# Storing a batch's ninth tokens by one transfer of 128 partitions, its DRAM side ordered half of the columns, token, column

## The chip, the cores and the metric

The kernel runs on one core of a Trainium2 chip. The metric is the device time of one execution in microseconds; lower is better. A core has a matrix engine (TensorE, PE in the profile, with its weight loads as PEld), three engines for elementwise work (VectorE or DVE, ScalarE or ACT, GpSimd or POOL), a SyncE (SP) that here issues nearly all transfers, and 16 DMA engines that move the data.

## The reference: thresholded attention, then a maxout feed-forward layer

```python
scores = scale * q @ k.T                       # 8 batches, 8 heads, 576 tokens, 64 columns
thresh = max(scores) - tau                     # by row
attn = softmax(where(scores >= thresh, scores, -1e9))
x = (attn @ v) with the heads side by side     # 4608 x 512
h = maximum(x @ w1, x @ w2, x @ w3)            # 4608 x 768
out = h @ w_out                                # 4608 x 512, float32
```

## The kernel before

A batch's 576 tokens are taken as 64 groups of 9: token 9p + c is number p of chunk c. Two chunks (c = 0 to 7) fill 128 rows, so a batch has four chunk pairs of 128 tokens and a ninth chunk (c = 8) of 64 tokens. Four heads are a "quad"; 8 batches of two quads give 16 quads.

For each quad q, k and v are loaded (`load`, lines 185-237) and q and k turned on TensorE (tiles tp, qt, kt). For each of nine steps the scores of 128 rows go to PSUM (`scores`, tile sc). VectorE takes the maximum, ScalarE and VectorE make the exponents and sums (tile z), GpSimd divides by the sums into a bf16 tile P (`normalized`, six buffers). A DMA transpose on SyncE's queue brings P's two heads into ptq (`turned`, lines 400-404), nine of them for a quad. When all nine have landed, TensorE multiplies ptq with v (`product`, lines 406-441, PSUM tile o, then xt). The last batch is taken in two parts, the first with only some of the steps.

The feed-forward layer of a batch (`ffn`, from line 466) has three steps. `hid` multiplies xt with the three weights (tiles ph, hm, hT). `outp` (lines 511-542) multiplies hT with w_out for two chunk pairs at a time (tile po), ScalarE copies 128 x 512 values to a buffer ob (four buffers) and SyncE stores 256 KB; the very last of these goes out on ScalarE's queue (q10 in the profile; SyncE's is q1). `ninth` (lines 544-565) does the same for the 64 ninth tokens: columns 0 to 255 of the output are made in PSUM rows 0 to 63 and columns 256 to 511 in rows 64 to 127, so ScalarE copies 128 x 256 values, to a buffer obr (two buffers). Row 64x + p of obr is thus half x of token p's row.

The order of all work is written out by hand in the string ORDER (lines 40-74), a letter for each piece, and `_Ordered` (lines 84-101) keeps each engine to it; that is why nearly every instruction of the profile carries line 93. N issues a ninth chunk's matmuls, j its copy, i its stores, and o a 256 KB store. Each of N, j and i occurs eight times, and the string ends with stores, i the last. The `store` of `ninth` is put off by way of the list stores9 until its i. A transfer waits, ahead of its issue on SyncE, for its data, and everything behind it in SyncE's order waits along.

Of the kernel before, what the change touches and what calls it, by code (L numbers as in the profile page):

```python
# [104 lines left out]
def kernel(  # L105
# [23 lines left out]
    tensor, scalar, vector, pool, sync = (  # L129
        _Ordered(tc, e) for e in (nc.tensor, nc.scalar, nc.vector, nc.gpsimd, nc.sync))  # L130
# [50 lines left out]
    def bank(name, where):  # L181
        return ps_s.tile([128, 1024], F32, name=name, tag=f"s{where}")
# [261 lines left out]
    def halves(banks):  # L444


        mine = []

        def issue(swap):
            if swap:  # L450

                gate = tensor.nop()
                tc.add_manual_dep(gate.ins, mine[0], mybir.DependencyInfo(mybir.DependencyClass.Sync, mybir.DependencyReason.DATA), reason="swap")
            for ms in zip(*banks):
                for h in (1, 0):
                    x = (1 - h) ^ swap
                    o, w, m = ms[x]
                    rows = slice(64 * h, 64 * h + 64)
                    last = tensor.matmul(o, w(rows), m(rows), start=(not swap and ms[x] is banks[x][0]),
                                         stop=(swap == 1 and ms[x] is banks[x][-1]))  # L460
            if not swap:
                mine.append(last.ins.name)

        return (lambda: issue(0)), (lambda: issue(1))

    def ffn(b, part):


        runs = ((0, S // 2), (S // 2, S)) if part is None else (span(part),)
        mine = [c for c in (part or range(5)) if c < 4]  # L470
        chunks = [tuple(mine[c:c + 2]) for c in range(0, len(mine), 2)] + ([4] if part is None or 4 in part else [])
        st = {}
        nr, n = len(runs), runs[0][1] - runs[0][0]

        def hid(f, wi):
            my = {}

            def operands(kc, a):
                c0, c1 = runs[a]
                return (my["ps"][:, a * 512:a * 512 + n],  # L480
                        lambda rows: wts[wi][rows, kc, f * 128:(f + 1) * 128],
                        lambda rows: x_of(b)[rows, kc, c0:c1])

            def first(where):
                my["ps"] = bank("ph", where)
                if nr == 1:
                    for kc in range(4):
                        o, w, m = operands(kc, 0)
                        tensor.matmul(o, w(slice(0, 128)), m(slice(0, 128)), start=(kc == 0), stop=(kc == 3))
                else:  # L490
                    my["h"] = halves([[operands(kc, a) for kc in range(4)] for a in range(2)])
                    my["h"][0]()

            def done():
                if wi == 0:
                    st["hm", f] = hp_.tile([128, nr, n], BF16, name="hm", bufs=3)
                hm = st["hm", f]
                pv = my["ps"].rearrange("p (a u) -> p a u", a=2)[:, :nr, :n]
                if wi == 0:
                    scalar.activation(out=hm, in_=pv, func=AF.Copy)  # L500
                else:
                    dst = hm if wi == 1 else \
                        h_of(b)[:, f, runs[0][0]:runs[-1][1]].rearrange("p (a u) -> p a u", a=nr)
                    vector.tensor_tensor(out=dst, in0=pv, in1=hm, op=OP.max)
            p = _Piece((b, part, f, wi), first, (lambda: my["h"][1]()) if nr == 2 else None, [done])
            p.kind = "v" if wi else "h"
            return p

        rows_out = out[b * S:(b + 1) * S, :].rearrange("(p c) m -> p c m", c=9)

        def outp(cs):

            my = {}
            c = cs[0]
            last = b == B - 1 and cs[-1] == 3

            def first(where):
                ps = bank("po", where)
                my["ps"] = two = [ps[:, 0:512], bank("po", (where + 2) % 4)[:, 512:1024] if last else ps[:, 512:1024]]
                if len(cs) == 1:  # L520
                    for f in range(NF):
                        tensor.matmul(ps[:, 0:512], h_of(b)[:, f, c * 128:c * 128 + 128], wo[:, f, :],
                                      start=(f == 0), stop=(f == NF - 1))
                    return
                my["h"] = halves([[(two[a],
                                    lambda rows, a=a, f=f: h_of(b)[rows, f, (c + a) * 128:(c + a) * 128 + 128],
                                    lambda rows, f=f: wo[rows, f, :]) for f in range(NF)] for a in range(2)])
                my["h"][0]()

            def done(a):  # L530
                ob = hp_.tile([128, DM], F32, name="ob", bufs=4)
                src = my["ps"][a]
                if last and a == 1:
                    vector.tensor_copy(out=ob, in_=src)
                    ends.append(lambda: scalar.dma_start(out=rows_out[:, (0, 2, 1, 3)[c + a]:8:4], in_=ob))
                    return
                scalar.activation(out=ob, in_=src, func=AF.Copy)
                stores.append(lambda: sync.dma_start(out=rows_out[:, (0, 2, 1, 3)[c + a]:8:4], in_=ob))
            p = _Piece((b, "out", c), first, (lambda: my["h"][1]()) if len(cs) == 2 else None,
                       [lambda a=a: done(a) for a in range(len(cs))])  # L540
            p.kind = "uf" if last else "u"
            return p

        def ninth():

            my = {}

            def first(where):
                my["ps"] = ps = bank("po", where)
                for f in range(NF):  # L550
                    for x in range(2):
                        tensor.matmul(ps[64 * x:64 * x + 64, :256], h_of(b)[:, f, 512:S], wo[:, f, 256 * x:256 * x + 256],
                                      start=(f == 0), stop=(f == NF - 1))

            def done():
                ob = hp_.tile([128, DM // 2], F32, name="obr", bufs=2)
                scalar.activation(out=ob, in_=my["ps"][:, :256], func=AF.Copy)

                def store():
                    for x in range(2):  # L560
                        sync.dma_start(out=rows_out[:, 8, 256 * x:256 * x + 256], in_=ob[64 * x:64 * x + 64])
                stores9.append(store)
            p = _Piece((b, "ninth"), first, None, [done])
            p.kind = "j"
            return p

        return ([hid(f, wi) for f in range(NF) for wi in range(3)],
                [outp(c) for c in chunks if c != 4], [ninth() for c in chunks if c == 4])
# [9 lines left out]
    def span(part):  # L578
        if part is None:
            return 0, S  # L580
        return 128 * part[0], S if part[-1] == 4 else 128 * part[-1] + 128
# [11 lines left out]
    def x_of(b):  # L593
        if b not in xts:
            xts[b] = xp.tile([128, 4, S], BF16, name="xt")
        return xts[b]

    def h_of(b):
        if b not in hTs:
            hTs[b] = hp_.tile([128, NF, S], BF16, name="hT")  # L600
        return hTs[b]
# [120 lines left out]
    x = 0  # L722
# [39 lines left out]
```

## Time and profile before

| | us |
|---|---|
| median of 3 runs | 449.69 (449.37 to 450.16) |
| the profiled execution | 448.81 |
| its span, first instruction to last | 447.0 |
| TensorE busy | 427.8 |
| ScalarE busy | 404.5 |
| VectorE busy | 391.4 |
| GpSimd busy | 310.7 |
| stores of obr | 16 of 64 KB, median 2.2 from issue to landing |
| DMA transposes | 144, median 4.6 from issue to landing |

All rows but the first are of one profiled execution. A row of the profile names the engine, the operation, and out<-in by the program's tiles; "SPq" is SyncE's sequencer, which issues transfers and waits. "Landing" is when a transfer's last completion is counted. The DMA view of a stretch of time counts the packets of all 16 DMA engines by size, and gives for each queue the time that its packets took as a share of 16 engines over the stretch; its row of digits is the busy share in tenths in 40 equal slices. The windows view gives the busy time of each engine in a stretch, then the granted clock of TensorE, the DMA share and GB/s.

### The profile page before, as it was taken

The page shows a single profiled execution, that of the slowest core. Times are in us where ns is not written, and L with a number is a line of the kernel's source. Part 1 is how long each engine was busy: PE and PEld are TensorE (multiplying, and loading weights), DVE is VectorE, ACT ScalarE, POOL GpSimd, SP SyncE. Part 2 cuts the span into 40 slices and gives each one's busy share as a digit, 9 for nine tenths or more (in the row PEclk, how much of TensorE's full clock was granted, in tenths as well). Part 3 has the DMA queues.
Part 4 walks back from the last instruction along what each step waited for, and adds up shares of the span by engine and source line. Part 5 has one row for each costly group of instructions (what it writes and reads, how often), then busy time and mean ns, then how long its engine had stood idle before and what let it go on. Part 6 is the DMA issues. An engine that isn't in the chain of part 4 may idle for free.

```text
span 447.0 us, 14312 instructions
## 1 busy us (share of the span) xinstructions
PE 427.8 (96%) x5188; PEld 320.1 (72%) x5188; DVE 391.4 (88%) x1225; ACT 404.5 (90%) x841; POOL 310.7 (70%) x420
## 2 busy tenths in 40 slices
PE   8777799999999999999999999999999999999995
PEld 6443545887787777788687776787688876786862
DVE  4988899989899999999899899999999998998542
ACT  3999999998999999999999999999999999898422
POOL 2799789998667875876767776687748784657200
PEclk9987789999999999999999999999999999999999
DMA  7999999999999999999989989989999996995812
GB/s 177 317 228 203 258 207 230 213 194 279 198 218 170 233 202 207 217 261 166 164 232 180 270 133 231 171 167 219 177 263 158 236 179 93 169 166 112 149 73 107
DMA packets 212840, 87.46 MB, mean 196 GB/s; under 512 B 185889, under 2 KB 199713, under 8 KB 212769
## 3 DMA queue, kind: packets, MB, share of 16 engines
q1 hardware_dynamic: 212320, 85.98, 96.2%
q8 instruction: 41, 0.67, 0.6%
q10 hardware_dynamic: 448, 0.56, 0.4%
q14 instruction: 31, 0.25, 0.2%
HBM read 34.60 MB, written 9.44 MB: 99 GB/s over the span
## 4 chain that ended last, share of the span: by engine, by line
PE 84%; ACT 5%; DVE 3%; POOL 3%; DMA 1%; issue 1%; SPq 1%; DVEq 0%; POOLq 0%
PE ph L93 32%; PE sc L93 30%; PE po L93 10%; PE o L93 9%; ACT z L93 4%; PE tp L93 3%; DVE z L93 2%; POOL P L93 2%; DMA qm<-in_q_dram 1%; SPq L93 1%; POOL qs L93 1%; DVE kt L93 0%; ACT qt L93 0%; POOL vb L93 0%; DVE stage L93 0%
## 5 line engine op out<-in xcount | busy, mean ns | idle before, releaser
L93 POOL TENSOR_SCALAR P<-z,rs 128x576 bf16<-128x576 f32 x250 | 197.8, 803 | 71.6 <-DVE rs L93 37.0
L93 DVE TENSOR_SCALAR_CACHE_REDUCE z<-sc 128x576 f32<-128x576 f32 x250 | 182.0, 752 | 19.8 <-PE sc L93 11.1
L93 PE MATMUL sc<-kt,qt 64*128 64x320 f32 (+2 forms) x640 | 184.0, 442 | 5.6 <-DVE z L93 3.2
L93 PE MATMUL sc<-kt,qs 64*128 64x256 f32 (+2 forms) x640 | 183.1, 430 | 6.2 <-ACT z L93 2.8
L93 PE MATMUL ph<-xt,w 64*128 64x288 bf16 (+2 forms) x2160 | 164.4, 283 | 0.0
L93 PEld LDWEIGHTS <-w 64*128 64x128 bf16 (+1 forms) x2160 | 127.0, 94 | 27.0 <-issue 4.2
L93 PEld LDWEIGHTS sc<-kt,qs 64*128 64x128 f32 (+1 forms) x640 | 95.7, 183 | 30.5 <-ACT z L93 7.5
L93 ACT ACTIVATE z<-z 128x576 f32<-128x576 f32 x170 | 114.6, 678 | 0.1
L93 PEld LDWEIGHTS sc<-kt,qt 64*128 64x128 f32 (+1 forms) x640 | 95.5, 183 | 20.9 <-DVE z L93 6.7
L93 ACT ACTIVATE z<-z,th 128x576 f32<-128x576 f32 x134 | 99.8, 769 | 2.3 <-DVE rs L93 1.5
L93 DVE SCALAR_TENSOR_TENSOR z<-z 128x576 f32<-128x576 f32 x80 | 62.9, 801 | 0.3 <-ACT z L93 0.3
L93 POOL COPY qs<-qt 64x640 f32<-64x640 f32 (+3 forms) x66 | 45.6, 691 | 14.5 <-ACT qt L93 11.1
L93 ACT ACTIVATE z<-z,nm 128x576 f32<-128x576 f32 x71 | 53.5, 767 | 0.0
L93 PE MATMUL po<-wo,hT 64*128 64x512 bf16 (+1 forms) x480 | 53.2, 356 | 0.1
L93 ACT ACTIVATE hm<-ph 128x576 bf16<-128x576 f32 (+2 forms) x54 | 31.8, 590 | 14.9 <-PE ph L93 14.6
L93 DVE TENSOR_TENSOR hm<-ph,hm 128x576 bf16<-128x576 f32 (+2 forms) x54 | 37.0, 686 | 9.4 <-PE ph L93 8.7
L93 POOL TENSOR_SCALAR P<-stage,rs 128x576 bf16<-128x576 f32 x38 | 29.9, 793 | 18.2 <-DVE rs L93 7.5
L93 PEld LDWEIGHTS <-hT 64*128 64x128 bf16 (+1 forms) x480 | 28.8, 97 | 17.0 <-issue 2.1
L93 DVE TENSOR_TENSOR hT<-ph,hm 128x576 bf16<-128x576 f32 (+2 forms) x54 | 37.1, 687 | 3.8 <-PE ph L93 1.3
L93 PE MATMUL o<-ptq,vb 128*64 128x64 bf16 (+2 forms) x544 | 38.6, 282 | 0.0
L93 ACT ACTIVATE z<-sc,nm 128x576 f32<-128x576 f32 x45 | 32.1, 746 | 4.3 <-DVE z L93 4.2
L93 ACT ACTIVATION_READ_ACCUMULATOR z<-z 128x1 f32 x170 | 33.4, 197 | 0.0
(42 smaller groups left out, 410.7 us busy)
## 6 DMA issues: line engine op xcount, KB each, us to landing
vm<-in_v_dram SPq DMA_DIRECT2D x32, 256.0 KB, 5.3
out_dram<-ob SPq DMA_DIRECT2D x31, 256.0 KB, 4.3
qm<-in_q_dram SPq DMA_DIRECT2D x15, 512.0 KB, 4.5
km<-in_k_dram SPq DMA_DIRECT2D x15, 512.0 KB, 5.3
stage<-in_moe_w_dram SPq DMA_DIRECT2D x9, 512.0 KB, 4.8
ptq<-P SPq DMA_TRANSPOSE x144, 4.6
stage<-in_moe_w_out_dram SPq DMA_DIRECT2D x3, 512.0 KB, 5.3
vr<-in_v_dram SPq DMA_DIRECT2D x32, 32.0 KB, 2.9
```

The source lines that it names most:

```text
L93: ins = fn(*a, **kw)
```

## The change

In `ninth`, the two stores of 64 partitions each (half x of the columns from rows 64x to 64x + 63 of obr) become one of all 128 partitions. Its source is the whole of obr; its destination is the same piece of the output, read in the order half of the columns (2), token (64), column (256). The bytes and where they go are the same, and so is everything else in the program: on every engine but SyncE the instructions stand in the same order as before, and on SyncE each pair of obr stores is one.

```diff
                 def store():
-                    for x in range(2):
-                        sync.dma_start(out=rows_out[:, 8, 256 * x:256 * x + 256], in_=ob[64 * x:64 * x + 64])
+                    sync.dma_start(out=rows_out[:, 8].rearrange("p (x m) -> x p m", x=2), in_=ob)
                 stores9.append(store)
```

Here `rows_out` is a batch's 576 output rows as [64 groups, 9, 512 columns]. A row of a half is 256 float32 values, 1 KB in one piece; neighbouring tokens of the chunk lie 18 KB apart in DRAM, and the two halves of a token 1 KB.

## The prediction

> **What bounds the kernel now.** I read the page first: the span, the busy shares and the chain that ended last.
>
> ```profile
> span 447.0 us, 14312 instructions
> PE 427.8 (96%) x5188; PEld 320.1 (72%) x5188; DVE 391.4 (88%) x1225; ACT 404.5 (90%) x841; POOL 310.7 (70%) x420
> ...
> PE 84%; ACT 5%; DVE 3%; POOL 3%; DMA 1%; issue 1%; SPq 1%; DVEq 0%; POOLq 0%
> ```
>
> TensorE is busy for 96% of the span and makes 84% of the chain; a transfer can matter in two ways only, by making TensorE wait or by standing behind its last work. The changed store stands there, so I read the chain near its end, then the timeline and the tile obr for the same stretch, and SyncE's waits.
>
> ```profile
> 442.62 0.38 ACT obr L93
> ```
>
> ```profile
> 442.54 0.54 SPq L93 DMA_DIRECT2D out_dram<-ob  x1
> 442.62 0.38 ACT L93 ACTIVATE obr<-po 128x256 f32<-128x256 f32 x1
> 442.68 0.64 ACTq L93 DMA_DIRECT2D out_dram<-ob  x1
> 443.17 1.28 SPq L93 DMA_DIRECT2D out_dram<-obr  x2
> ```
>
> ```profile
> L93 SPq DMA_DIRECT2D out_dram<-obr x2: 552/614/675, 443.2 to 443.8; - x2
> ...
> DMA to landing us min/median/max: 2.2/2.4/2.7
> ```
>
> ```profile
> SPq L757 <- DMA out_dram<-obr: 1.5, 1, 1.5
> ```
>
> The last arithmetic is the copy of the last batch's ninth tokens out of PSUM. It ends at 443.00, SyncE issues the two stores at 443.17 and 443.78, and they land 2.7 and 2.2 us later, at 445.9 and 446.0. SyncE waits 1.5 us for them, and the span ends 1.0 us after the landing. So **the last pair of stores is on the path that sets the end**, microsecond for microsecond. The other seven pairs are issued while TensorE works.
>
> **The change part by part.** It removes eight of SyncE's issues and leaves the bytes, the packets and the arithmetic as they are: still 64 + 64 rows of 1 KB. What it alters is the shape of the output side, which now begins with a dimension of 2 in place of one of 64. How a transfer is dealt out to the 16 DMA engines can be counted where nothing else runs, in the DMA view of 438 to 447 us, with six stores (four of 256 KB, two of 64 KB).
>
> ```profile
> DMA packets 737, 1.20 MB, mean 133 GB/s; under 512 B 96, under 2 KB 224, under 8 KB 736
> ```
>
> The 224 - 96 = 128 packets of 1 KB are the two small stores' rows, 736 - 224 = 512 of 2 KB the other four's. The 96 tiny ones are 16 for each of the six transfers, one for each engine: a store of 64 rows is dealt 4 rows to an engine, one of 128 rows 8. Each of them leads with 64 or 128 on both sides, which 16 divides; so does every other transfer of the kernel. The new store leads with 128 in SBUF and with 2 in DRAM, and no row shows such a one. The ends are 16 engines, as in these rows, and 2, one for each leading piece. The rows are nearer to 16, but they share just the property that the change takes away: with 16 engines, one side's leading dimension would have to be cut in mid-dimension to keep both sides in step. I take **2 engines**, and keep 16 as a rival.
>
> The Trainium skill, "DMA: Bandwidth & Descriptors", section "Why a DMA increments its semaphore by 16 and not by 1", says that a transfer issued by SyncE uses the largest number of engines up to 16 that divides the slowest dimension (other than 1) of both sides. The 16 small packets for each transfer agree with it; for 128 and 2 it gives 2. No run here shows that case yet.
>
> **At the end.** What do 64 rows on one engine cost? Two stretches hold such packets nearly alone: 445.15 to 446 us, behind the last stores, and 383.7 to 385 us, with a pair in mid-run.
>
> ```profile
> DMA packets 143, 0.11 MB, mean 129 GB/s; under 512 B 36, under 2 KB 143, under 8 KB 143
> ...
> q1 hardware_dynamic: 139, 0.11, 40.4%
> ```
>
> ```profile
> DMA packets 167, 0.13 MB, mean 102 GB/s; under 512 B 39, under 2 KB 167, under 8 KB 167
> ...
> q1 hardware_dynamic: 167, 0.13, 39.3%
> ```
>
> In the first, 107 rows took at most 0.404 x 16 x 0.85 = 5.5 us, 51 ns each, the tiny packets counted in; I take 48 for a row alone. In the second, 128 rows took 0.393 x 16 x 1.3 = 8.2 us, 64 ns each. So 64 rows on one engine take 3.1 us (64 x 48 ns) to 4.1 us (64 x 64), where the 8 of now take 0.4. They queue behind the two 256 KB stores of the timeline, as the DMA view of 443.6 to 447 shows:
>
> ```profile
> DMA  0489999999999999998999300000000000000000
> ...
> q1 hardware_dynamic: 304, 0.39, 32.3%
> q10 hardware_dynamic: 144, 0.26, 20.8%
> ```
>
> A slice is 0.085 us. The engines are busy from 443.69 to 445.6 without a gap; each has 0.323 x 3.4 = 1.10 us of q1 and 0.208 x 3.4 = 0.71 us of q10. With 0.4 of it gone and 3.1 put in, the two engines are done at 443.69 + 1.81 - 0.4 + 3.1 = 448.2, where the last is done at 445.6 now: 2.6 us later, and 3.6 by 64 ns. The two needn't be the ones that are last now, so I take **2.5 us**. The issue that goes (0.61 us, the median above) brings nothing there: the first of the pair is issued at the same 443.17, and its rows wait for the engines. If nothing stood ahead of them, rows could start at most 445.1 - 444.4 = 0.7 us earlier (1.2 us behind the issue, as the 442.54 store's behind its own), so the smallest gain in time, with all rows at 48 ns, would be a loss of still 1.9 us.
>
> **In mid-run.** Each of the seven other stores puts 56 rows more, 2.7 us (56 x 48 ns), on two engines, and what is issued next lands later by up to that, less 0.6 us of issue saved. What follows are DMA transposes, for which TensorE's products wait. The tightest place is the second pair:
>
> ```profile
> 307.39 1.99 SPq L93 DMA_DIRECT2D out_dram<-obr  x2
> 309.49 7.09 SPq L93 DMA_TRANSPOSE ptq<-P  x5
> ```
>
> ```profile
> DMA to landing us min/median/max: 3.3/3.6/5.3
> ```
>
> ```profile
> 321.24 1.15 PE L93 MATMUL o<-ptq,vb 128*64 128x512 bf16 x16
> ```
>
> ```profile
> 309.00:317.00 8.00, 8.00 (x95) 5.24 (x93) 7.67 (x25) 8.00 (x18) 4.44 (x7) 1.00 1.06 199
> ```
>
> The middle row is that of the transposes issued from 309 to 320 us. The five take 1.42 us each (7.09 / 5), so the fifth is issued at about 315.2 (309.49 + 4 x 1.42) and landed by 320.5 at the latest (5.3 us); its product starts at 321.24, so 0.7 us of cover. The DMA share of 1.06 says that the engines have no slack there to work off a backlog. At the worst 2.7 - 0.6 (issue) - 0.7 (cover) = 1.4 us reach TensorE; at the best nothing, as the two engines catch up whenever they finish a transpose in less than SyncE's 1.42 us. I take 0. Elsewhere the cover is larger:
>
> ```profile
> 237.86 1.24 SPq L93 DMA_DIRECT2D out_dram<-obr  x2
> 239.20 3.32 SPq L93 DMA_TRANSPOSE ptq<-P  x2
> ```
>
> ```profile
> 251.09 0.65 PE L93 MATMUL o<-ptq,vb 128*64 128x512 bf16 x6
> ```
>
> ```profile
> 389.43 1.24 SPq L93 DMA_DIRECT2D out_dram<-obr  x2
> 390.77 1.27 SPq L93 DMA_TRANSPOSE ptq<-P  x1
> 392.14 0.59 SPq L93 DMA_DIRECT2D out_dram<-ob  x1
> 392.82 3.17 SPq L93 DMA_TRANSPOSE ptq<-P  x2
> ```
>
> ```profile
> 401.49 0.63 PE L93 MATMUL o<-ptq,vb 128*64 128x256 bf16 x8
> ```
>
> ```profile
> 420.97 2.53 SPq L93 DMA_DIRECT2D out_dram<-obr  x4
> 423.54 1.89 SPq L93 DMA_DIRECT2D out_dram<-ob  x3
> ```
>
> Behind the first pair the transposes are issued by 242.5, and with the 5.3 us from above they land by 247.8, 3 us ahead of their product; behind the pair at 389.43 the first two, which the product at 401.49 reads, are issued by 394.4 and land by 399.7, 1.8 us ahead by the worst landing. The two pairs from 420.97 have only stores behind them, which no arithmetic reads; the two obr buffers are written again only by the second ninth chunk after.
>
> **Sum.** 2.5 us at the end, 0 in mid-run: a span of 449.5 in place of 447.0, and 451.3 in place of the profiled execution's 448.81 (1.8 us lie around its span). That execution was 0.9 us below the median of the runs, 449.69; I put the same step on the median: **452.2**.
>
> **Rivals.** *All 16 engines, not slower.* If the transfer is dealt out by its 128 rows, each engine gets the same 8 rows as now, one issue of 0.61 us goes, and the end stays with engines that are busy to 445.6 anyway: 0 to 0.6 us gained, 449.1 to 449.7, likeliest 449.5. It decides at one point: whether the last landing stays at 446.0 or earlier. For it speak the 16 packets of each transfer in the row above, against it that none leads with fewer than 16. A sentence of the Trainium skill speaks for such a gain: "DMA: Bandwidth & Descriptors", section "Rules for kernel authors", advises one 128-partition transfer in place of two on disjoint halves of the partitions, as both halves use the same engines. The rows agree in that both stores of a pair use all 16, but the rule takes for granted that the merged one does too.
>
> *The backlog reaches TensorE.* As the forecast, and at 321.24 up to 1.4 us more, with as much again where several delays meet (389 us): 453.5 to 455. For it speaks the DMA share of 1.06, against it the covers above.
>
> *The rows are slower on two engines.* 64 ns a row instead of 48: 453.2. It is the upper end of the forecast.
>
> *It is cut into the two old transfers again*, with both issues: 449.7.
>
> **How the numbers follow.** Forecast with its own range 451.2 to 453.4: 0.72. Backlog on TensorE: 0.13. Sixteen engines: 0.12, two thirds of it within 0.2%. Cut in two: 0.03. The range, 451.2 to 454.8, takes in the first and the second and leaves out 0.15 for the cases near 449.5. A measurement of this kernel tells about 0.2% (0.9 us) from no change. Faster by more: 0.03; within: 0.12; slower by more: 0.85.
>
> **What would show it.** In the window of the last five stores the tiny packets fall from 96 to 4 x 16 + 2 = 66 with two engines, to 80 with sixteen. The last obr store takes about 5.2 us to land instead of 2.2 to 2.7, and SyncE's last wait for it grows from 1.5 to about 4.6 us. The product at 321.24 starts with no wait for ptq. I am wrong if the last landing stays near 446.0, or if the last copy of obr, at 442.62, comes later by over 0.5 us.

## The result, and the profile after

The changed kernel takes **453.23 us** (median of 10 runs, 451.17 to 456.36) against 449.75 (10 runs, 448.47 to 450.22): ratio **1.0082**, 95% interval 1.0057 to 1.0108. It is slower by 2.6 to 4.9 us. The profiled execution took 453.22 us, with a span of 451.4.

The page after, its span and busy shares, and the chain's shares:

```profile
span 451.4 us, 14301 instructions
PE 427.2 (95%) x5188; PEld 320.3 (71%) x5188; DVE 390.6 (87%) x1225; ACT 404.3 (90%) x841; POOL 309.6 (69%) x420
...
PE 84%; ACT 6%; POOL 3%; DVE 2%; DMA 2%; issue 1%; SPq 0%; POOLq 0%; DVEq 0%
```

No engine has more work: TensorE's busy time is 427.2 us where it was 427.8, yet the span is 4.4 us longer. So look at the end. The timeline behind the last matmuls:

```profile
443.65 0.38 ACT L93 ACTIVATE obr<-po 128x256 f32<-128x256 f32 x1
443.65 0.64 ACTq L93 DMA_DIRECT2D out_dram<-ob  x1
444.20 0.54 SPq L93 DMA_DIRECT2D out_dram<-obr  x1
```

and what SyncE waited for in the same stretch:

```profile
SPq L756 <- DMA out_dram<-obr: 5.6, 1, 5.6
```

The copy ends at 444.03 and the span at 451.4: 7.4 us, where it was 443.00 to 447.0, 4.0 us. SyncE's wait for the last store grew from 1.5 to 5.6 us. The DMA view of 440 to 452 us, with its busy digits and GB/s in slices of 0.3 us, says why:

```profile
DMA  0200006979910001999990111011111000000000
GB/s 0 55 0 0 0 0 239 396 273 362 416 62 0 0 0 48 362 416 403 403 120 17 27 21 24 34 48 48 48 48 48 34 24 14 0 0 0 0 0 0
DMA packets 707, 1.20 MB, mean 100 GB/s; under 512 B 66, under 2 KB 194, under 8 KB 706
```

Five stores left 66 tiny packets: 16 for each of the four stores of 256 KB and **2 for the merged store**. Its 194 - 66 = 128 rows are the plateau at the right: digit 1 (two engines of sixteen) and 48 GB/s falling to 24, where one engine is done, after 400 GB/s for the stores ahead of it.

The other 1.0 us of the longer span is there before the change can act. The first matmuls of three products, at 122, 200 and 424 us, after:

```profile
122.52 1.22 PE L93 MATMUL o<-ptq,vb 128*64 128x512 bf16 x15
...
200.99 1.18 PE L93 MATMUL o<-ptq,vb 128*64 128x512 bf16 x16
...
425.57 0.63 PE L93 MATMUL o<-ptq,vb 128*64 128x256 bf16 x8
```

and before:

```profile
122.34 1.22 PE L93 MATMUL o<-ptq,vb 128*64 128x512 bf16 x15
...
199.95 1.18 PE L93 MATMUL o<-ptq,vb 128*64 128x512 bf16 x16
...
424.54 0.63 PE L93 MATMUL o<-ptq,vb 128*64 128x256 bf16 x8
```

After is 0.18 us late at 122, 1.04 at 200 and 1.03 at 424. The first changed store is issued at 238.6 us, behind all of that delay; from there on, through seven merged stores, TensorE loses nothing. The product that the prediction called the tightest, at 321.24 before, is 1.03 us late too and waits for nothing:

```profile
322.27 1.16 PE L93 MATMUL o<-ptq,vb 128*64 128x512 bf16 x16
```

### The profile page after: what moved, and what is told of

It reads as the page before. It is cut to its first block, busy times and chain, and to the rows that moved or that the text cites. A ratio compares the mean times of both kernels' runs of the same rounds, so it can differ in the third digit from the quotient of the medians.

```text
span 451.4 us, 14301 instructions
## 1 busy us (share of the span) xinstructions
PE 427.2 (95%) x5188; PEld 320.3 (71%) x5188; DVE 390.6 (87%) x1225; ACT 404.3 (90%) x841; POOL 309.6 (69%) x420
## 4 chain that ended last, share of the span: by engine, by line
PE 84%; ACT 6%; POOL 3%; DVE 2%; DMA 2%; issue 1%; SPq 0%; POOLq 0%; DVEq 0%
PE ph L93 31%; PE sc L93 31%; PE po L93 10%; PE o L93 9%; ACT z L93 5%; PE tp L93 3%; DMA qm<-in_q_dram 2%; POOL P L93 2%; DVE z L93 1%; POOL qs L93 1%; DVE kt L93 0%; ACT qt L93 0%; SPq L93 0%; POOL vb L93 0%; DVE stage L93 0%
```

## The experiments

Theory A: the whole loss is the last store, dealt to two engines, on the path to the end; the seven in mid-run are covered. The main rival, B: the seven hold up DMA transposes and TensorE waits for them. "The end" below is the time from the end of the last copy of obr to the end of the span, 4.0 us before and 7.4 after. It is the sharpest measure: within one kernel's runs the whole times differ by 1.8 us and more.

**Only the last store merged** (e1_last_only) and **only the first seven** (e2_first_seven), each against before:

```diff
-                    for x in range(2):
-                        sync.dma_start(out=rows_out[:, 8, 256 * x:256 * x + 256], in_=ob[64 * x:64 * x + 64])
+                    if b == B - 1:      # e2: if b < B - 1
+                        sync.dma_start(out=rows_out[:, 8].rearrange("p (x m) -> x p m", x=2), in_=ob)
+                    else:
+                        for x in range(2):
+                            sync.dma_start(out=rows_out[:, 8, 256 * x:256 * x + 256], in_=ob[64 * x:64 * x + 64])
```

> Only the last of the eight ninth stores is one transfer; the first seven stay pairs. Theory A (the whole loss is the last store, dealt to two engines, on the path to the end; the seven in mid-run are covered): as the changed kernel, 3.0 to 3.8 us over before, about 453.1. Rival B (the seven delay transposes and TensorE waits, the last store is only a part of the loss): 1 to 2.5 us over before. In the DMA view of the last 11 us the tiny packets are 66 by both.

> The first seven ninth stores are one transfer each, the last stays a pair. Theory A: as before, within 0.5 us of 449.75. Rival B: 1 to 2.5 us over before, with TensorE's waits for ptq, or the distance between the two kernels' matmuls, growing behind one of the stores.

The last alone: 453.97 us against 449.53, ratio 1.0102 (1.0079 to 1.0126); the end 7.3 us, with 66 tiny packets. The first seven alone: 449.72, ratio 1.0007 (0.9985 to 1.0029); the end 4.1 us. The spans and the last copies of the two, the last alone first:

```profile
span 451.7 us, 14311 instructions
...
443.96 0.38 ACT L93 ACTIVATE obr<-po 128x256 f32<-128x256 f32 x1
```

```profile
span 447.0 us, 14302 instructions
...
442.50 0.38 ACT L93 ACTIVATE obr<-po 128x256 f32<-128x256 f32 x1
```

In the profile of the first seven alone, the first products behind the first and the second merged store (before, at 251.09 and 321.24):

```profile
250.97 1.18 PE L93 MATMUL o<-ptq,vb 128*64 128x512 bf16 x16
...
321.12 1.16 PE L93 MATMUL o<-ptq,vb 128*64 128x512 bf16 x16
```

Both are 0.12 us early, as this execution was already at 200 us (199.83): between and behind two merged stores nothing was lost.

Theory A holds for the place of the loss, and B falls: the last store alone costs 3.6 to 5.7 us by the interval, the seven nothing that can be told from zero. In size A gave 3.0 to 3.8 us; the end is 3.3 us longer (7.3 - 4.0), but the medians differ by 4.4. That profile was 1.4 us late before 200 us, with no changed instruction until 444. Whether such a delay makes the rest of the medians' difference too isn't shown.

**How many engines: 61, 62 and 60 tokens in the last pair** (e3_last_61, e3_last_62, e3_last_60), to see what decides it without any leading 2:

```diff
+                    n = 61 if b == B - 1 else 64      # 62, 60
                     for x in range(2):
-                        sync.dma_start(out=rows_out[:, 8, 256 * x:256 * x + 256], in_=ob[64 * x:64 * x + 64])
+                        sync.dma_start(out=rows_out[0:n, 8, 256 * x:256 * x + 256], in_=ob[64 * x:64 * x + n])
```

> The last pair stores 61 of its 64 tokens, in two transfers of 61 partitions (three tokens of the last batch are left out of the output). Theory A in its narrow form (a transfer uses the largest number of engines up to 16 that divides its leading dimension): 61 has no divisor but 1, so both transfers, 122 rows, run on one engine: 122 x 48 ns = 5.9 us, to 122 x 56 = 6.8, where 8 rows take 0.4: 5.2 to 6.4 us over before, and 4 x 16 + 2 x 1 = 66 tiny packets in the last 11 us. Rival C (it was the 2 pieces of the output side; rows are shared out over 16 engines as evenly as they go): as before, 96 tiny packets.

> The last pair stores 62 of its 64 tokens, two transfers of 62 partitions (two tokens of the last batch are left out of the output). Theory A: 62 gives 2 engines, 31 rows each, 62 on each engine for the pair: the end like the merged store's, 6.5 to 7.5 us from the last copy's end to the end of the span (7.4 with one transfer), 3 to 4 us over before, 68 tiny packets in the last 11 us. Rival C (the cost comes of the output side's leading 2, not of the number of engines): as before, 4.0 us behind the last copy.

> The last pair stores 60 of its 64 tokens, two transfers of 60 partitions (four tokens of the last batch are left out of the output). Theory A (the largest divisor up to 16 of the leading dimension): 60 gives 15 engines, 4 rows each: the end as before, 4.0 us from the last copy's end to the end of the span, and 4 x 16 + 2 x 15 = 94 tiny packets in the last 11 us. Rival C (any leading dimension that 16 doesn't divide drops to one or two engines): 6 to 10 us behind the last copy.

The packet counts of the last stretch, with 61, 62 and 60 tokens (the DMA views of 440 to 457, 438 to 452 and 438 to 449 us):

```profile
DMA packets 701, 1.19 MB, mean 70 GB/s; under 512 B 66, under 2 KB 188, under 8 KB 700
```

```profile
DMA packets 705, 1.19 MB, mean 85 GB/s; under 512 B 68, under 2 KB 192, under 8 KB 704
```

```profile
DMA packets 727, 1.19 MB, mean 108 GB/s; under 512 B 94, under 2 KB 214, under 8 KB 726
```

With 64 of them for the four larger stores, 2, 4 and 30 are left for the two small ones: 1, 2 and 15 engines each, the largest divisors up to 16 of 61, 62 and 60.

| last store | engines | the end, us | median, us | ratio to before beside it (interval) |
|---|---|---|---|---|
| pair of 64 (before) | 16 | 4.0 | | |
| pair of 60 | 15 | 3.9 | 449.82 | 0.9991 (0.9974 to 1.0008) |
| pair of 62 | 2 | 7.8 | 453.44 | 1.0079 (1.0056 to 1.0103) |
| merged (after) | 2 | 7.4 | 453.23 | 1.0082 (1.0057 to 1.0108) |
| pair of 61 | 1 | 10.3 | 457.03 | 1.0166 (1.0134 to 1.0198) |

So it is the number of engines and not the merging or the leading 2 as such: one token fewer than 62 costs 2.5 us more at the end, two fewer cost nothing against before. All three expectations of C fall. Theory A held for the engines in each; in size, the pair of 62 was 0.3 us over the end forecast for it, and the pair of 61 has an end 6.3 us longer than before's, within the 5.2 to 6.4 forecast, but a median 7.5 us over its before of 449.53 (its profile was 3.4 us late at 200 us).

The Trainium skill's rule that the prediction named ("DMA: Bandwidth & Descriptors", "Why a DMA increments its semaphore by 16 and not by 1") agrees with all five counts.

**Twice the dose in mid-run** (e5_seven_61): the same edit with `if b < B - 1` and 61, so that each of the first seven pairs puts 122 rows on one engine.

> The first seven pairs store 61 of 64 tokens each (three tokens of seven batches are left out of the output); the last pair is whole. A test of the cover in mid-run with twice the dose: if 61 rows go to one engine, each pair puts 122 x 48 = 5.9 us on one engine where the merged store put 3.1 on each of two. Theory A with the covers of the prediction: the product behind the second pair has 0.7 us of cover, so up to 5 us of wait there, with catching up 1 to 5 us over before in all. Rival D (a backlog on one engine in mid-run is hidden whatever its size): within 0.5 us of before.

457.91 us, ratio 1.0182 (1.0151 to 1.0213): 6.8 to 9.6 us, more than either expectation. The end is 4.0 us, and the profile, 0.96 us behind before's at 200 us, is 9.12 behind it at 424: 8.2 us arise in mid-run. TensorE's waits for transfers from 237 us on and the product behind the second pair, whose first matmul before is at 321.24:

```profile
PE o L93 <- DMA ptq<-P: 4.0, 3, 2.2
PE tp L93 <- DMA qm<-in_q_dram: 1.5, 1, 1.5
```

```profile
323.91 0.38 PE L93 MATMUL o<-ptq,vb 128*64 128x512 bf16 x1
325.88 0.44 PE L93 MATMUL o<-ptq,vb 128*64 128x512 bf16 x3 [1.58 <-DMA ptq<-P]
```

The product starts, waits 1.58 us for a transpose and goes on. After and the first seven alone have no such wait from 237 us to the end. So the cover is real and finite: 64 rows on each of two engines fit under it, 122 on one don't. Rival D falls. The place called the tightest makes only 1.8 us of the loss; 1.7 are lost behind the first pair, where TensorE waits for a load of q (tile qm), 0.7 behind the third (at 354 us of before) and 4.0 behind the fifth (402 to 405). What was left out can be read in SyncE's timeline, the five transposes behind the second store, with 61 tokens in the first fence and in the changed kernel in the second (7.09 us before):

```profile
310.58 12.40 SPq L93 DMA_TRANSPOSE ptq<-P  x5
```

```profile
308.22 0.58 SPq L93 DMA_DIRECT2D out_dram<-obr  x1
308.90 9.40 SPq L93 DMA_TRANSPOSE ptq<-P  x5
```

Rows crowded on one or two engines don't only let transfers land later; the transposes behind them also take SyncE longer to issue, which the prediction had left at its pace. Most of it is in one transpose, as a rule the first: behind each of the first five stores of the changed kernel one transpose takes 2.6 to 3.4 us to issue, with 61 tokens 4.7 to 5.0; the transposes in these places took 1.3 to 1.9 before. The 256 KB stores that stand between (at 384.58 and 385.31 us in the changed kernel) are issued in some 0.6 us as before. What in the transpose has to wait isn't shown.

**Why a row took 56 ns and not 48** (e8_load_ahead). In the changed kernel's last store the rows took 0.112 x 16 x 4.0 = 7.2 us for 128, 56 ns each (DMA view of 446.1 to 450.1 us):

```profile
DMA packets 145, 0.14 MB, mean 35 GB/s; under 512 B 13, under 2 KB 141, under 8 KB 145
...
q1 hardware_dynamic: 130, 0.13, 11.2%
```

In its packet records most rows take 46 ns, but 9 take 74 to 239, all begun within 3.3 us of the issue. The experiment issues a 512 KB load ahead of the last merged store:

```diff
+                    if b == B - 1:
+                        t = stage.tile([128, 4 * 256], F32, name="stage")
+                        sync.dma_start(out=t.rearrange("p (k f) -> p k f", k=4), in_=moe_w1[:, 0:256].rearrange("(ko p) f -> p ko f", p=128))
                     sync.dma_start(out=rows_out[:, 8].rearrange("p (x m) -> x p m", x=2), in_=ob)
```

> All eight stores merged as in the change; the last has a 512 KB load, which nothing reads, issued ahead of it, so that its rows find the DMA engines busy for longer. Asked: why the 64 rows on an engine took 3.9 us and not 3.1. Theory F (rows are slow only in the first 3.3 us behind the issue, while the transfer is still being set up for its two engines): the rows start over 2.5 us behind the issue, all at 46 ns, and take 3.0 us from first to last. Rival G (two engines writing alone, or reading the same half of SBUF, are slower for long): some 3.9 us again, with rows of 150 to 240 ns among them.

The store is issued at 446.52; its rows alone are in the DMA view of 450.4 to 452.9 us:

```profile
DMA packets 113, 0.11 MB, mean 45 GB/s; under 512 B 2, under 2 KB 113, under 8 KB 113
...
q1 hardware_dynamic: 113, 0.11, 12.8%
```

0.128 x 16 x 2.5 = 5.1 us for 111 rows, 46 ns each, none over (one profiled execution). G falls: two engines write at full pace alone.

The rows were slow early behind the issue, as F says, but the early rows of the last store also share the engines with ScalarE's 256 KB store, and here the load kept them apart from that too. The mid-run stores of the changed kernel, which have no store of ScalarE's queue beside them, decide between the two. In the packet records the rows of those issued at 238.61, 342.21 and 383.88 begin 1.2 to 1.3 us behind the issue and take 55, 62 and 55 ns on the mean, single ones up to 387. Those of the stores at 308.22 and 391.89 begin 2.5 and 2.9 us behind it and take 46 on the mean, none over 70. So the slow rows go with the time since the issue, as F says, though 3.3 us is no sharp bound: two slow rows of the store at 342.21 begin 3.6 and 4.6 us behind it. That a set-up makes the rows slow is argued only. Nor is it the merged store's rows alone: four 2 KB rows of ScalarE's store took 687 to 916 ns in the same stretch, and none over 186 in the three profiles of before. The end with the load is 8.6 us, as the load itself stands in the way.

**Two tries at a shorter end.** One transfer of 64 partitions with 2 KB rows (e4_last_wide):

```diff
+                if b == B - 1:
+                    wide = hp_.tile([128, DM], F32, name="ob", bufs=4)
+                    vector.tensor_copy(out=wide[0:64, 256:512], in_=my["ps"][64:128, :256])
+                    scalar.activation(out=wide[0:64, 0:256], in_=my["ps"][0:64, :256], func=AF.Copy)
+                    stores9.append(lambda: sync.dma_start(out=rows_out[:, 8], in_=wide[0:64]))
+                    return
```

> The last ninth store is one transfer, but of 64 partitions with 2 KB rows: ScalarE and VectorE copy a half each to a 64 x 512 buffer; the first seven stay pairs. Theory A (the engines are what costs, one issue in place of two is worth nothing at the end, since the DMA engines are busy with the 256 KB stores): 16 engines, the end as before or at most 0.6 us earlier, 449.0 to 449.8. Rival H (one big transfer of this batch lands late for another reason, such as the single issue): 2 us or more over before.

and the second half of the last pair on ScalarE's queue (e6_two_queues):

```diff
-                        sync.dma_start(out=rows_out[:, 8, 256 * x:256 * x + 256], in_=ob[64 * x:64 * x + 64])
+                        (scalar if x and b == B - 1 else sync).dma_start(out=rows_out[:, 8, 256 * x:256 * x + 256], in_=ob[64 * x:64 * x + 64])
```

> As before, but the second half of the last pair is issued on ScalarE's queue, so that the two halves are issued beside each other; an attempt at a shorter end than either kernel's. Theory A: all 16 engines, the rows wait for the 256 KB stores anyway; from the last copy's end to the end of the span 3.4 to 4.0 us where before has 4.0. Rival (two queues at once slow each other): 4.3 or more.

The wide store: 450.31 us, ratio 1.0011 (0.9992 to 1.0029), 80 tiny packets (16 engines for each of five stores). From the last matmul to the end of the span it has 4.37 us, before 4.45. So one transfer of the same 128 KB on 16 engines costs nothing: rival H falls, and the merged store's price is the engines. The median is somewhat over A's 449.0 to 449.8, and no different from the 449.96 of its before. In its timeline the two copies don't run side by side:

```profile
444.62 0.38 ACT L93 ACTIVATE ob<-po 64x256 f32<-64x256 f32 x1 [0.62 <-DVE ob L93]
```

ScalarE's copy waits 0.62 us for VectorE's. It ends 0.94 us behind the last matmul, where before's ends 0.42 behind it; from there to the end of the span it is 3.4 us and not 4.0. What the single issue would be worth with no such wait isn't shown. The two queues: 450.24 us against 448.91, ratio 1.0025 (1.0006 to 1.0044), the end 4.1 us, between the two expectations: no gain, and the 1 us more in the medians stands nowhere in its end (its profile was 1.3 us late at 200 us). Neither beats the kernel before.

**Before, twice more** (before_again, before_third), for the delay ahead of 200 us:

> The kernel before, unchanged, profiled once more. Asked: the profiles so far differ by 0 to 3.4 us in the time at which TensorE reaches the same matmul, all of it gathered before 180 us, where all kernels are the same. If that is a difference between executions, this profile shows some of it too, none behind 180 us, and again 4.0 us from the last copy's end to the end of the span. If it comes of the changed stores, this profile stands within 0.2 us of the first.

> The kernel before, unchanged, profiled a third time, with the same question: by the first reading 0.3 to 3 us later or earlier somewhere ahead of 180 us; by the second within 0.2 us of the first profile.

The end is 4.1 and 4.0 us, and spans are 447.1 and 448.7 us. The third's products at the same places as above:

```profile
122.09 1.22 PE L93 MATMUL o<-ptq,vb 128*64 128x512 bf16 x15
...
201.63 1.18 PE L93 MATMUL o<-ptq,vb 128*64 128x512 bf16 x16
...
426.24 0.63 PE L93 MATMUL o<-ptq,vb 128*64 128x256 bf16 x8
```

The unchanged kernel is 0.25 us early at 122, 1.68 late at 200 and 1.70 late at 424. The second profile is 0.53 us early at 122 and 0.05 late at 200, within the 0.2 us of the other reading; the third is what tells them apart. So delays larger than the 1.0 us of the first comparison come about with no changed store at all. The first profile of before is one of the quick ones, as its 448.81 us against a median of 449.7 says. What makes the delays isn't settled. The kernels with a slow last store stood 0.3 to 3.4 us late at 200 us (five profiles) and those with an unslowed end -0.1 to 1.9 (eight); that doesn't tell them apart.

## Why the prediction was right, point by point

- **The direction and the place** held. The last store is on the path to the end, microsecond for microsecond: the last store alone gives the whole loss.
- **Two engines** held, to the packet: 66 tiny packets were forecast and counted. The choice was made against the nearer rows, and the rival of 16 engines is refuted by the same count, and that of two old transfers by it and by the one issue, x1, in the timeline.
- **2.5 us at the end** was too small: 7.4 - 4.0 = 3.4 us. Mis-sized was the row on one engine, taken at 48 ns. It measured 56 ns on the mean, with the slow rows right behind the issue, so the rows took 3.9 us and not 3.1 on the engine that ended last; the 0.1 us taken off because the two engines needn't be the last fell away. The prediction's dearer bound of 64 ns, 3.6 us, was the nearer one. That its 453.2 us is the time measured is luck: it stands for rows that are all slower, and most took 46 ns.
- **Nothing in mid-run** held for the time; its working held in part. The tight product, at 321.24 before, is at 322.27 after: 1.03 us late, as it already was at 200. But the five transposes ahead of it took SyncE 9.40 us to issue and not 7.09, so the catching up that the prediction counted on isn't what hid the backlog. They also began earlier: at 308.90, which is 307.87 on before's clock, 1.6 us ahead of before's 309.49, as the pair took SyncE 1.99 us and the merged store 0.58. So the issue of the last of them ends 0.7 us later than before, and that fits under the cover. The cover was taken at 0.7 us by the worst landing; in before's profile the fifth transpose lands at 319.96, 1.3 us ahead of the product.
- **The step on the median**: the longer end of 3.4 us, put on the median of 449.69, gives 453.1, and 453.23 was measured. The spans of the two profiles alone would have given 4.4 us, of which 1.0 was there before the first changed store.
- **What would show it** came in part: the wait for the last store grew to 5.6 us, not 4.6, and the product at 321.24 had no wait for ptq. One sign of being wrong came too: the last copy of obr, at 442.62 before, started at 443.65, 1.03 us later where 0.5 was the bound. That sign was badly chosen. All of the 1.03 us is there at 200 us, ahead of the first changed store, and the unchanged kernel's third profile has its copy 1.70 us later; the sign took a difference between executions for one of the change.

## What to carry to other kernels

Before merging transfers, look at the outermost dimension of both sides as the transfer will carry it: 64 rows twice ran on 16 engines each, the same 128 rows with a leading 2 on the DRAM side on two. Count the tiny completion packets in a quiet stretch of the DMA view: one for each engine of each transfer. Compare two profiles by the time of the same instruction along the span, and look where a difference arises, before it is put down to a change. A transfer behind the last arithmetic is paid in full, while the same transfer in mid-run costs nothing until its backlog is larger than the cover of the tightest product behind it, and then quickly a lot: 8.2 us over seven stores with about twice the rows on an engine.

## What the runs showed of the hardware

- Most rows of 1 KB to DRAM took 46 ns on a DMA engine, in the last pair of before with 16 engines as in the merged store with 2. In the merged store, rows begun up to 3.3 us behind the issue took up to 239 ns at the end of the changed kernel, later ones 46.
- A transfer from SyncE led by 64, 60, 62 or 61 on both sides ran on 16, 15, 2 or 1 DMA engines by its tiny packets, and one led by 128 and 2 on 2.
- Behind stores that put many rows on one or two engines, transposes on SyncE's queue take longer to issue: five of them took 7.09 us with the pair on 16 engines, 9.40 with 64 rows on each of two, 12.40 with 122 rows on one.
